# Attention in a fused attention and expert kernel: two heads' scores in row halves, the output scaled in place of P, and a planned order

## The chip, the core and the metric

The kernel runs on one core of a Trainium2 chip. The metric is the device time of one execution in microseconds. The engines are TensorE (PE, with its weight loads PEld), VectorE (DVE), ScalarE (ACT), GpSimd (POOL) and SyncE (SP, which here only issues DMAs).

## What is computed

Block-causal attention over 4 batches of 8 heads, sequence 576, head size 64; then a two-layer softplus network on the 2304 rows, and a routed expert network. Only the first part is touched by the change:

```python
def _attn_ref(q, k, v) -> np.ndarray:
    B, H, S, D = q.shape
    block = 64
    scale = 1.0 / np.sqrt(D)
    scores = scale * np.matmul(q, k.transpose(0, 1, 3, 2))
    ...
    mask = block_i >= block_j
    scores = np.where(mask, scores, -1000000000.0)
    scores = scores - np.max(scores, axis=-1, keepdims=True)
    attn = np.exp(scores)
    attn = attn / (np.sum(attn, axis=-1, keepdims=True) + 1e-09)
    return np.matmul(attn, v).astype(np.float32)
...
    attn_out = _attn_ref(**attn_kwargs)
    x = np.ascontiguousarray(attn_out.transpose(0, 2, 1, 3)).reshape(B * S, H * D)
    x = _moe_ref(x=x, **moe_kwargs)
    return _moe2_ref(x=x, **moe2_kwargs)
```

## The kernel before

Attention works on 16 pairs of heads (`NPAIR`), one pair after the other, overlapped. A pair's q and k come as rows of 128 positions with both heads side by side; `transposes_qk` (L281) turns them with PE into a PSUM tile `tp`, so that head 0 lies on partitions 0 to 63 and head 1 on 64 to 127. `evacuate_qk` (L295) copies them with ACT into `rq` and `rk` (scaling q), and `split_qk` (L306) makes a rounded high part and the remainder, the low part, with ACT, POOL and DVE. The q parts go into `bd`, a block diagonal: for each of the 9 blocks of 64 queries a 128 x 128 matrix with head 0's queries in one corner and head 1's in the other and zeros elsewhere.

`scores` (L376) computes a block's scores for both heads at once, 128 rows (2 heads x 64 queries), with only the keys that the block may see (64 for block 0, 576 for block 8), in three passes (high x high, high x low, low x high) into PSUM tiles `s`, four of one bank each; DVE takes the negated maximum (L389). `exps` (L403) writes P = exp(s - max) with ACT and its row sums; `denominators` and `reciprocals` are small DVE operations; `normalise` (L430) multiplies P by the reciprocals, on DVE for eight blocks and on POOL for block 5. `transposes_p` (L440) turns P with PE into `tp` (three banks), `evacuate_p` (L452) copies it to `pt` with ACT, block 3 with DVE. `values` (L472) multiplies by v: 32-bit matmuls with 64 output rows for each head, head 0 into PSUM partitions 0 to 63 and head 1 into 64 to 127; queries 0 to 255 and 256 to 575 are two halves in one bank each in turn, each computed in two calls. `evacuate_v` (L491) copies the output to `xT` with ACT.

Between these steps each pair converts a piece of the 64-bit expert weights (`convert_piece`, L230: POOL, DVE, ACT) and loads the next.

The order in which instructions are issued is written by hand: `WHEN` gives each step a place in units of a block (nine for a pair), `FIRST` and `LAST` shift single steps of the first three pairs and the last; everything is sorted by place, and each engine executes its instructions in that order. The tile framework adds the semaphore waits. The start of pair 0 has its own functions (`start_first`, L336, with tile 0 alone, and `start_rest`, L349), with filler matmuls (`keep_busy`, L330) between the first transposes: 15, twice 8 and twice 3. At the end `split_x`, `split_w`, `layer1` and `softplus` of the next stage are given places beside the last pair's steps.

## Time and profile before

| | us |
|---|---|
| median of 3 runs (lowest, highest) | 727.8 (725.16, 728.51) |
| the profiled execution | 724.71 |
| its span, first to last instruction | 723.0 |
| PE, DVE, ACT, POOL busy | 691.8, 521.3, 385.8, 268.3 |

The page gives each engine's busy time as a share of the span, the span in 40 slices with the clock granted to PE in tenths of full speed, and groups of instructions by source line. Busy time of PE is a union of overlapping records, so a busy PE need not be at its peak. Time in a stage is better read from distances between starts in the timeline, and idle time from the brackets there, which name what ended it.

### The profile page before, as it was taken

How to read it: one execution, taken by the hardware profiler on the slowest of the kernel's cores; microseconds unless marked ns; L12 is line 12 of the kernel's file. 1: busy time of each engine (PE TensorE's matmuls, PEld its weight loads, DVE VectorE, ACT ScalarE, POOL GpSimd, SP SyncE). 2: the span in 40 equal slices, each digit the busy share in tenths (PEclk: the TensorE clock that was granted, in tenths of full speed). 3: DMA queues.
4: the chain of work that ended last, by engine and by line, in shares of the span. 5: the costliest groups of instructions: out<-in, count | busy, mean ns of one | idle time of the engine just before them, and what ended most of it. 6: DMA issues, size and time to landing. Idle time of an engine off the chain costs nothing. (4 is left out here: it accounts for less than half of the span.)

```text
span 723.0 us, 11570 instructions
## 1 busy us (share of the span) xinstructions
PE 691.8 (96%) x3966; PEld 535.3 (74%) x3966; DVE 521.3 (72%) x1172; ACT 385.8 (53%) x964; POOL 268.3 (37%) x237
## 2 busy tenths in 40 slices
PE   7999999999998999999999999999999999986996
PEld 6777777777766788888888888888888677775742
DVE  6889999999999986568755788667674365574322
ACT  5788888888886565556445344544453232320111
POOL 6567787778757642312121122112110020113220
PEclk8899999999999999999999999999999999999999
DMA  6434252433220110012101011110001140985620
GB/s 155 92 96 97 70 124 66 102 91 91 70 76 27 33 58 30 29 38 67 41 31 58 1 59 59 48 41 29 1 1 52 66 117 1 319 307 167 241 77 11
DMA packets 86197, 56.76 MB, mean 79 GB/s; under 512 B 65102, under 2 KB 74318, under 8 KB 86128
## 3 DMA queue, kind: packets, MB, share of 16 engines
q1 hardware_dynamic: 84832, 53.68, 25.5%
q0 software_dynamic: 1296, 2.24, 1.0%
q8 instruction: 33, 0.54, 0.3%
q14 instruction: 36, 0.29, 0.1%
HBM read 45.11 MB, written 10.92 MB: 78 GB/s over the span
## 5 line engine op out<-in xcount | busy, mean ns | idle before, releaser
L546 PE MATMUL h<-xs,wi 128*128 128x512 f32 (+1 forms) x960 | 215.8, 373 | 1.6 <-DVE xs L527 1.2
L546 PEld LDWEIGHTS h<-xs,wi 128*128 128x128 f32 x960 | 168.5, 188 | 38.0 <-DVE xs L527 1.5
L598 PE MATMUL o<-wo,gh 128*128 128x512 f32 x576 | 182.9, 398 | 0.2 <-DVE wo L535 0.2
L561 DVE SCALAR_TENSOR_TENSOR e<-h,e 128x512 f32<-128x512 f32 (+1 forms) x80 | 50.8, 636 | 103.0 <-ACT e L559 102.4
L598 PEld LDWEIGHTS o<-wo,gh 128*128 128x128 f32 x576 | 106.3, 188 | 23.9 <-DVE wo L535 0.7
L258 POOL TENSOR_TENSOR cc<-cc,cb 128x512 f32<-128x512 f32 (+1 forms) x40 | 44.1, 1101 | 201.9 <-DVE cb L255 157.0
L557 ACT ACTIVATE e<-h 128x512 f32<-128x512 f32 (+1 forms) x80 | 44.3, 553 | 132.3 <-PE h L546 132.3
L598 PE MATMUL o<-wo,gl 128*128 128x512 f32 x288 | 113.9, 396 | 0.0
L411 ACT ACTIVATE p<-s,mx 128x288 f32<-128x288 f32 (+8 forms) x160 | 80.1, 509 | 17.1 <-DVE mx L389 14.1
L434 DVE TENSOR_SCALAR p<-p,sm 128x64 f32<-128x64 f32 (+7 forms) x128 | 77.0, 623 | 0.0
L445 PE MATMUL tp<-ident,p 128*128 128x128 f32 x384 | 70.1, 288 | 5.9 <-DVE p L434 2.9
L389 DVE TENSOR_REDUCE mx<-s 128x1 f32<-128x288 f32 (+8 forms) x160 | 66.3, 442 | 9.0 <-PE s L385 8.9
L567 DVE TENSOR_TENSOR gl<-e,gh 128x512 fp32r<-128x512 f32 (+1 forms) x80 | 65.9, 823 | 6.8 <-DVE gh L566 0.5
L729 POOL DMA_INDIRECT lst<-pay,si x18 | 17.8, 988 | 126.1 <-DVE pay L722 79.3
L598 PEld LDWEIGHTS o<-wo,gl 128*128 128x128 f32 x288 | 54.2, 188 | 13.2
L445 PEld LDWEIGHTS tp<-ident,p 128*128 128x128 f32 x384 | 42.6, 142 | 26.8 <-issue 9.4
L466 ACT ACTIVATE pt<-tp 128x512 f32<-128x512 f32 (+3 forms) x128 | 57.7, 471 | 4.2 <-PE tp L445 4.0
L485 PE MATMUL v<-pt,vr 128*64 128x320 f32 (+4 forms) x448 | 59.3, 374 | 0.5 <-PE s L385 0.5
L566 DVE CAST gh<-e 128x512 fp32r<-128x512 f32 (+1 forms) x80 | 43.8, 547 | 6.7 <-PE o L598 0.5
L558 ACT ACTIVATE e<-e 128x512 f32<-128x512 f32 (+1 forms) x80 | 47.2, 590 | 2.5
L559 ACT ACTIVATE e<-e 128x512 f32<-128x512 f32 (+1 forms) x80 | 47.2, 590 | 2.5
L485 PEld LDWEIGHTS v<-pt,vr 128*64 128x64 f32 (+1 forms) x448 | 25.2, 135 | 23.8 <-issue 12.8
(240 smaller groups left out, 1098.5 us busy)
## 6 DMA issues: line engine op xcount, KB each, us to landing
xs<-in_moe_w_dram SPq DMA_DIRECT2D x16, 512.0 KB, 6.9
raw<-in_moe_w_in_dram SPq DMA_DIRECT2D x12, 512.0 KB, 3.7
raw<-in_moe_w_out_dram SPq DMA_DIRECT2D x12, 512.0 KB, 3.2
xd<-xT SPq DMA_DIRECT2D x18, 256.0 KB, 2.7
out_dram<-xT SPq DMA_DIRECT2D x18, 256.0 KB, 3.5
vr<-in_v_dram SPq DMA_DIRECT2D x32, 128.0 KB, 2.6
qr<-in_q_dram SPq DMA_DIRECT2D x30, 128.0 KB, 3.0
kr<-in_k_dram SPq DMA_DIRECT2D x30, 128.0 KB, 2.6
```

The lines of the kernel that those rows point to most:

```text
L389: nc.vector.tensor_reduce(out=mx[:, si:si + 1], in_=ps[:, 0:e - a], axis=AX.X, op=ALU.max, negate=True)
L411: nc.scalar.activation(out=pn[i][:, a:e], in_=pss[si][:, 0:e - a], func=AF.Exp, bias=nm, accum_out=sm[:, 0, c + si:c + si + 1])
L434: eng.tensor_scalar(out=pt, in0=pt, scalar1=sums[p, g][:, 2, c:c + 1], scalar2=None, op0=ALU.mult)
L445: nc.tensor.transpose(ps[:, j].rearrange("p h q -> p (h q)"), src[:, j * P:(j + 1) * P], ident)
L466: nc.scalar.activation(out=dst, in_=ps[:, 0:nfull], func=AF.Copy)
L485: nc.tensor.matmul(out=ps[h * D:(h + 1) * D, c0 - q0:q1 - q0], lhsT=vt[0:rows, kt, h, :], rhs=rhs, start=(kt == 0), stop=(kt == nk - 1), s ...
L546: nc.tensor.matmul(out=ps[:, 0:n], lhsT=a[:, kc, :], rhs=b[:, 0:n], start=(kc == 0 and j == 0), stop=(kc == KC - 1 and j == 2),)
L558: nc.scalar.activation(out=e[:, 0:n], in_=e[:, 0:n], func=AF.Exp, scale=-1.0)
L559: nc.scalar.activation(out=e[:, 0:n], in_=e[:, 0:n], func=AF.Ln, bias=1.0)
L561: nc.vector.scalar_tensor_tensor(out=g[:, 0:n], in0=ps[:, 0:n], scalar=0.0, in1=e[:, 0:n], op0=ALU.max, op1=ALU.add)
L567: nc.vector.tensor_tensor(out=gl[:, 0:n], in0=g[:, 0:n], in1=gh[:, 0:n].bitcast(F32), op=ALU.subtract)
L598: nc.tensor.matmul(out=acc[c, t], lhsT=a[:, ts], rhs=b, start=(fc == f0 and j == 0), stop=(fc == f1 - 1 and j == 2),)
```

## The change

Queries are taken in four tiles of 128 for one head each, and a tile of 64 + 64 (`TAIL`) for the last 64 queries of both heads.

- **Scores.** For tiles 0 to 3, head 0's matmul uses partitions 0 to 63 (row half one of the array) and head 1's 64 to 127, each with 128 queries, into separate banks of a two-bank PSUM tile; there are two such tiles in place of four single banks, and tile 1 shares that of tile 0. All keys up to the end of the tile are computed; a small bf16 matmul (`unseen` x `ones`) adds -2^33 to the last 64 keys for the first 64 queries. The remainder stays a block diagonal of 64 + 64 queries.
- **Splitting.** `split_high` (ACT) and `split_low` (DVE) read q and k from the PSUM tile; `rq`, `rk` and the POOL and DVE splits go.
- **Scaling.** P is no longer scaled. The reciprocals of a pair (18 columns: high and low parts of 9) are transposed by PE, copied by ACT, spread over 64 partitions each by five matmuls with `spread`, copied by ACT into the place of the output in `xT`, and DVE multiplies the output of P V by them in place of the ACT copy.
- **PSUM.** `tp` has two banks, not three; `va` and `vb` one each for the two halves of P V. P V of the first half is one call.
- **Order.** Steps have costs, needs, buffers and due times; a list scheduler works the order out when the kernel is built. `convert_piece` is cut into five steps, the load of the next piece follows the third. Setup memsets go to POOL; `setup_routing` and the routing loads become steps. The start has 15 filler matmuls and no functions of its own.

```diff
-    ps_t = second.enter_context(tc.tile_pool(name="ps_t", bufs=3, space=PSUM))
+    ps_t = second.enter_context(tc.tile_pool(name="ps_t", bufs=2, space=PSUM))
-    ps_s = first.enter_context(tc.tile_pool(name="ps_s", bufs=4, space=PSUM, side="right"))
+    ps_s = first.enter_context(tc.tile_pool(name="ps_s", bufs=2, space=PSUM, side="right"))
...
-    bd = [[qt_p.tile([P, NB, 2, BLK], F32R, name=f"bd{i}{w}") for w in "hl"] for i in range(2)]
-    kt = [[qt_p.tile([P, S], F32R, name=f"kt{i}{w}") for w in "hl"] for i in range(2)]
-    rq = qt_p.tile([P, S], F32, name="rq")
-    rk = qt_p.tile([P, S], F32, name="rk")
+    TAIL = FULL
+    qs = [[qt_p.tile([P, FULL * P], F32R, name=f"q{i}{w}") for w in "hl"] for i in range(2)]
+    ks = [[qt_p.tile([P, S], F32R, name=f"k{i}{w}") for w in "hl"] for i in range(2)]
+    bd = [[qt_p.tile([P, 2, REM], F32R, name=f"bd{i}{w}") for w in "hl"] for i in range(2)]
+
+    unseen = qt_p.tile([P, P], BF16, name="unseen")
+    UNSEEN = -2.0 ** 33
+
+    spread = pt_p.tile([2 * (2 * FULL + 1), TT, P], F32R, tag="spread", name="spread")
+    NR = 2 * FULL + 1
...
+    def split_of(p, part):
+
+        ps = tq[p, part]
+        (qh, ql), (kh, kl), (bh, bl) = qs[p % 2], ks[p % 2], bd[p % 2]
+        lo, hi = (P, FULL * P) if p == 0 else (0, FULL * P)
+        if part == 0:
+            return [(ps[:, lo:hi], qh[:, lo:hi], ql[:, lo:hi], True)]
+        if part == 1:
+            return [(ps[:, lo:hi], kh[:, lo:hi], kl[:, lo:hi], False)]
+        if part == 3:
+            return [
+                (ps[:, 0:P], qh[:, 0:P], ql[:, 0:P], True), (ps[:, P:2 * P], kh[:, 0:P], kl[:, 0:P], False),
+            ]
+        rows = [slice(h * D, (h + 1) * D) for h in range(2)]
+        return [(ps[r, 0:REM], bh[r, h, :], bl[r, h, :], True) for h, r in enumerate(rows)] + [
+            (ps[:, REM:2 * REM], kh[:, FULL * P:S], kl[:, FULL * P:S], False)
+        ]
+
+    def split_high(p, part):
+        for x, hi, _, is_q in split_of(p, part):
+            nc.scalar.activation(out=hi, in_=x, func=AF.Copy, scale=scale if is_q else 1.0)
+
+    def split_low(p, part):
+        for x, hi, lo, is_q in split_of(p, part):
+            if is_q:
+                nc.vector.scalar_tensor_tensor(
+                    out=lo, in0=x, scalar=scale, in1=hi.bitcast(F32), op0=ALU.mult, op1=ALU.subtract
                 )
-
-    def evacuate_qk(p, part):
-        ps = tq.pop((p, part))
-        if part < 2:
-            nc.scalar.activation(
-                out=(rq, rk)[part][:, 0:FULL * P], in_=ps[:, 0:FULL * P], func=AF.Copy,
-                scale=scale if part == 0 else 1.0,
+            else:
+                nc.vector.tensor_tensor(out=lo, in0=x, in1=hi.bitcast(F32), op=ALU.subtract)
+
+
...
+    def columns(t):
+        return slice(P, 3 * P) if t == 1 else slice(0, (t + 1) * P)
+
+    def scores(p, t):
+        (qh, ql), (kh, kl), (bh, bl) = qs[p % 2], ks[p % 2], bd[p % 2]
+        if t != 1:
+            sc_ps[p, t] = ps_s.tile([P, 2, 512], F32, tag="s", name="s"), st_p.tile([P, 4], F32, tag="mx", name="mx")
+        else:
+            sc_ps[p, 1] = sc_ps[p, 0]
+        ps, mx = sc_ps[p, t]
+        if t == TAIL:
+            for k0, n in ((0, FULL * P), (FULL * P, REM)):
+                for j, (x, y) in enumerate(((bh, kh), (bh, kl), (bl, kh))):
+                    nc.tensor.matmul(
+                        out=ps[:, int(k0 > 0), 0:n], lhsT=x.rearrange("p h q -> p (h q)"), rhs=y[:, k0:k0 + n],
+                        start=(j == 0), stop=(j == 2),
+                    )
+            return
+        cs = columns(t)
+        n = (t + 1) * P
+        last_keys = slice(cs.stop - BLK, cs.stop)
+        heads = [slice(h * D, (h + 1) * D) for h in range(2)]
+        for j, (x, y) in enumerate(((qh, kh), (qh, kl), (ql, kh))):
+            for h, r in enumerate(heads):
+                nc.tensor.matmul(
+                    out=ps[:, h, cs], lhsT=x[r, t * P:(t + 1) * P], rhs=y[r, 0:n], start=(j == 0), stop=False,
+                )
+        for h, r in enumerate(heads):
+            nc.tensor.matmul(out=ps[:, h, last_keys], lhsT=unseen[r, :], rhs=ones[r, 0:BLK], start=False, stop=True)
+
+    def maxima(p, t):
+
+        ps, mx = sc_ps[p, t]
+        if t == TAIL:
+            nc.vector.tensor_reduce(
+                out=mx[:, 0:1], in_=ps.rearrange("p h n -> p (h n)")[:, 0:S], axis=AX.X, op=ALU.max, negate=True
             )
         else:
...
+            c = 2 * int(t == 1)
+            nc.vector.tensor_reduce(
+                out=mx[:, c:c + 2], in_=ps[:, :, columns(t)], axis=AX.X, op=ALU.max, negate=True
             )
 
...
-    def normalise(p, i):
-        g, c = divmod(i, GROUP)
-        pt = pn[i][:, 0:BLK * (i + 1)]
-        eng = nc.gpsimd if i in POOL_NORM else nc.vector
-        eng.tensor_scalar(out=pt, in0=pt, scalar1=sums[p, g][:, 2, c:c + 1], scalar2=None, op0=ALU.mult)
...
+    def exps(p, t, h):
+        ps, mx = sc_ps[p, t]
+        if p not in sums:
+            sums[p] = st_p.tile([P, 2, NR], F32, tag="sm", name="sm", bufs=2)
+        x = ps.rearrange("p h n -> p (h n)")[:, 0:S] if t == TAIL else ps[:, h, columns(t)]
+        c = 2 * int(t == 1) + h
+        nc.scalar.activation(
+            out=pn[t, h], in_=x, func=AF.Exp, bias=mx[:, c:c + 1], accum_out=sums[p][:, 0, 2 * t + h:2 * t + h + 1]
+        )
+
+    rr = {}
+
+    def reciprocals(p):
+
+        sm = sums.pop(p)
+        t = rr[p] = st_p.tile([P, 2 * NR], F32R, tag="rr", name="rr", bufs=2)
+        nc.vector.tensor_scalar(out=sm[:, 1, :], in0=sm[:, 0, :], scalar1=1e-9, scalar2=None, op0=ALU.add)
+        nc.vector.reciprocal(out=sm[:, 0, :], in_=sm[:, 1, :])
+        nc.vector.tensor_copy(out=t[:, 0:NR], in_=sm[:, 0, :])
+        nc.vector.tensor_tensor(out=t[:, NR:2 * NR], in0=sm[:, 0, :], in1=t[:, 0:NR].bitcast(F32), op=ALU.subtract)
+
 
...
+    def rows_of_reciprocals(p):
+        nc.tensor.transpose(pv[p, 0][0:2 * NR, HALF:HALF + P], rr.pop(p).bitcast(F32), ident)
+
+    def keep_rows(p):
+        rs[p] = st_p.tile([2 * NR, P], F32R, tag="rT", name="rT", bufs=2)
+        nc.scalar.activation(out=rs[p], in_=pv[p, 0][0:2 * NR, HALF:HALF + P], func=AF.Copy)
+
+    def spread_reciprocals(p):
+
+        ps = pts[p, "r"] = ps_t.tile([P, 512], F32, tag="tp", name="tp")
+        r = rs.pop(p)
+        for t in range(FULL):
+            nc.tensor.matmul(out=ps[:, t * P:(t + 1) * P], lhsT=spread[:, t, :], rhs=r, start=True, stop=True)
+        nc.tensor.matmul(
+            out=pv[p, 0][:, HALF:HALF + P], lhsT=spread[:, TAIL, :], rhs=r, start=True, stop=True,
+            skip_group_check=True,
+        )
+
+    def x_of(p, q0, q1):
         b, hp = divmod(p, NP)
-        q0, q1 = ((0, HALF), (HALF, S))[half]
-        ps = pv.pop((p, half))
-        nc.scalar.activation(out=xT[:, hp, b * S + q0:b * S + q1], in_=ps[:, 0:q1 - q0], func=AF.Copy)
-
-    POOL_NORM = (5,)
-    DVE_EVAC = (3,)
-    SPLIT = "apv"
+        return xT[:, hp, b * S + q0:b * S + q1]
+
+    def keep_reciprocals(p):
+
+        nc.scalar.activation(out=x_of(p, 0, FULL * P), in_=pts.pop((p, "r")), func=AF.Copy)
+        for h in range(2):
+            r = slice(h * D, (h + 1) * D)
+            nc.scalar.activation(
+                out=x_of(p, FULL * P, S)[r], in_=pv[p, 0][r, HALF + h * REM:HALF + (h + 1) * REM], func=AF.Copy
+            )
+
+    def normalise(p, half):
+        q0, q1 = queries(half)
+        x = x_of(p, q0, q1)
+        nc.vector.tensor_tensor(out=x, in0=pv[p, half][:, 0:q1 - q0], in1=x, op=ALU.mult)
+
+    DVE_EVAC = ((2, 0),)
...
-        for kt in (range(0, nk // 2), range(nk // 2, nk))[part]:
+        for kt in ((range(0, nk),), (range(0, 2), range(2, nk)))[half][part]:
...
-    keep_busy(KBS[0])
+    keep_busy(15)
     make_identity(nc, ident)
-    nc.vector.memset(one, 1.0)
+    nc.gpsimd.memset(unseen, 0.0)
+    for h in range(2):
+        nc.gpsimd.memset(unseen[h * D:h * D + 1, 0:BLK], UNSEEN)
     for i in range(2):
         for w in range(2):
-            (nc.vector, nc.gpsimd)[w].memset(bd[i][w].bitcast(F32), 0.0)
-    for i in range(0, NB - 1, 2):
-        nc.vector.memset(pn[i][:, BLK * (i + 1):BLK * (i + 2)], 0.0)
-    nc.vector.memset(blank[:, :, :, 0], NT)
-    nc.vector.memset(blank[:, :, :, 1], 0)
-    start_first()
-    setup_routing()
-    U = [(p, i) for p in range(NPAIR) for i in range(NB)]
-
-
-    WHEN = {
-        "normalise": [-0.81, -0.02, 0.8, 1.94, 1.97, 3.13, 4.51, 4.77, 7.37],
-        "scores": [-6.89, -6.43, -4.94, -3.99, -2.29, -1.47, -1.32, 0.65, 0.7],
-        "exps": [-5.21, -5.15, -3.6, -1.61, -1.5, -0.44, 2.3, 2.53, 3.31],
-        "transposes_p": [1.22, 1.93, 2.47, 3.48, 4.44, 5.39, 7.03, 7.17, 8.93],
-        "evacuate_p": [2.76, 3.14, 3.74, 4.46, 4.67, 6.89, 8.1, 8.24, 9.45],
-        "join_max": [-5.42, -5.73, -4.17, -3.32, -1.63, -0.68, 1.47, 0.65, 0.87],
-        "denominators": [-3.03, -0.18, 3.44],
-        "reciprocals": [-1.53, 0.23, 3.89],
-        "values": [6.98, 8.34, 10.92, 12.28],
-        "evacuate_v": [9.2, 12.74],
-        "load_qk": [-22.26],
-        "load_v": [-1.76],
-        "transposes_qk": [-19.2, -16.06, -14.87],
-        "evacuate_qk": [-16.53, -14.84, -14.77],
-        "split_qk": [-11.11, -12.62, -8.78],
-        "convert": [1.05, 10.91, 15.45],
+            nc.gpsimd.memset(bd[i][w].bitcast(F32), 0.0)
+
+    nc.gpsimd.memset(zeros, 0.0)
+    nc.gpsimd.memset(blank[:, :, :, 0], NT)
+    nc.gpsimd.memset(blank[:, :, :, 1], 0)
...
+    DUE = {
+        "ldqk": [-30.0], "ldv": [-14.0], "T": [-17.0, -16.0, -15.0, -18.0], "H": [-15.5, -14.5, -13.5, -17.5],
+        "L": [-15.0, -14.0, -13.0, -17.0], "S": [-6.0, -5.5, -4.0, -2.0, 0.0], "M": [-5.5, -5.0, -3.5, -1.5, 0.5],
+        "E": [-5.0, -4.5, -3.0, -1.0, 1.0], "TP": [0.0, 1.0, 2.0, 4.0, 6.0], "EV": [0.5, 1.5, 2.5, 4.5, 6.5],
+        "EV5": [7.0], "V": [3.0, 8.5], "R": [2.0], "RT": [8.5], "RK": [8.6], "RM": [9.0], "RX": [9.2],
+        "N": [10.2, 10.3], "C": [8.0, 9.0, 10.0, 11.0, 12.0],
+
...
+        while could:
+            now = [(t, s) for t, s in ((ready(s, free), s) for s in could) if t is not None]
+            at, best = min(now, key=lambda x: x[0])
+            e = best.parts[0][0]
+            at, best = min(
+                ((t, s) for t, s in now if s.parts[0][0] == e and t <= at + SLACK), key=lambda x: x[1].due
+            )
...
+        for t in range(TT):
+            if t == TAIL:
+                needs = [k("L", i) for i in range(3)]
+                parts = pe(3 * S, b=0.1)
+            else:
+                needs = [k("L", 3)] if p == 0 and t == 0 else [k("L", i) for i in ((3, 0, 1) if p == 0 else (0, 1))]
+                parts = pe(3 * (t + 1) * P + BLK, b=0.15)
+            before = k("S", t - 1) if t else ("S", p - 1, TAIL)
+            if before in steps_of:
+                needs.append(before)
+            add("S", (t,), parts, scores, needs)
+            n = S if t == TAIL else 2 * (t + 1) * P
+            add("M", (t,), dve(n), maxima, [k("S", t)])
+            for h in range(1 if t == TAIL else 2):
+                add("E", (t, h), act(S if t == TAIL else (t + 1) * P, True), exps, [k("M", t)])
...
+        for t in (0, 2, 3, TAIL):
+            ring("s", 2, k("S", t), [e for e in E if e[2] == t or (t == 0 and e[2] == 1)])
...
+        add("R", (), [("DVE", 0.6)], reciprocals, E, args=())
+        add("RT", (), pe(128, 0.86, 0.05), rows_of_reciprocals, [k("R"), k("V", 0, 0)], args=())
+        add("RK", (), act(128), keep_rows, [k("RT")], args=())
+        add("RM", (), pe(576, 0.4535, 0.15), spread_reciprocals, [k("RK"), k("V", 0, 0)], args=())
+        add("RX", (), [("ACT", 0.75)], keep_reciprocals, [k("RM")], args=())
+        add("N", (0,), dve(256), normalise, [k("RX"), k("V", 0, 0)])
+        add("N", (1,), dve(320), normalise, [k("RX"), k("V", 1, 1)])
+        ring("tp", 2, k("RM"), [k("RX")])
+        ring("va", 1, k("V", 0, 0), [k("N", 0), k("RX"), k("EV5")])
+        ring("vb", 1, k("V", 1, 0), [k("N", 1)])
+
...
+    step("spread", [("POOL", 3.0)], setup_spread, (), 5.0)
+    steps_of["RM", 0].needs.append("spread")
+    step("setup", [("POOL", 5.0), ("DVE", 1.0)], setup_routing, (), 12.0)
+    firsts.append("setup")
+    step("load_routing", [("SP", 1.0)], load_routing, ["setup"], PACE + 5.0)
+    step("move", [(None, 0.0)], move_on, firsts + ["load_routing"])
...
+    for kc, (a, b) in enumerate((("DVE", "POOL"), ("DVE", "POOL"), ("DVE", "POOL"), ("DVE", "POOL"))):
+        step(
+            ("x1", kc), [(a, cost_of[a]), (b, cost_of[b])],
+            lambda kc=kc, a=a, b=b: split_x(1, kc, engine[a], engine[b]),
+            [("TP", z) + x for x in of_page[kc]], end + 8 + kc,
+        )
...
+    for s in in_order():
+        s.do()
```

## Rows read from the trace of the kernel before

**Rows 1.** The page, busy us, share of the span and instructions of each engine.
```profile
PE 691.8 (96%) x3966; PEld 535.3 (74%) x3966; DVE 521.3 (72%) x1172; ACT 385.8 (53%) x964; POOL 268.3 (37%) x237
```
**Rows 2.** The page, granted clock in 40 slices of 18 us, tenths of full speed.
```profile
PEclk8899999999999999999999999999999999999999
```
**Rows 3.** Stretches: us, busy us (instructions) of PE, PEld, DVE, ACT, POOL, clock, DMA.
```profile
8.00:16.00 8.00, 6.24 (x30) 5.69 (x30) 4.87 (x11) 4.64 (x18) 4.88 (x4) 0.67 0.81 202
...
24.00:32.00 8.00, 8.00 (x49) 6.54 (x48) 5.43 (x16) 5.67 (x18) 4.15 (x3) 0.76 0.65 142
...
103.10:115.60 12.50, 12.46 (x96) 9.45 (x94) 12.05 (x34) 11.00 (x37) 9.73 (x9) 1.00 0.39 93
...
128.11:141.62 13.51, 12.67 (x96) 9.47 (x94) 12.83 (x36) 10.99 (x37) 9.45 (x9) 1.00 0.36 90
```
**Rows 4.** Timeline, one pair: start us, us, engine, instruction, count, idle before.
```profile
100.31 0.14 PEld L445 LDWEIGHTS tp<-ident,p 128*128 128x128 f32 x1 [0.49 <-DVE p L434]
...
112.81 0.14 PEld L445 LDWEIGHTS tp<-ident,p 128*128 128x128 f32 x1 [0.49 <-DVE p L434]
...
100.83 0.28 PE L385 MATMUL s<-kt1h,bd1h 128*128 128x64 f32 x1
100.94 0.28 PE L385 MATMUL s<-kt1l,bd1h 128*128 128x64 f32 x1
...
101.61 0.28 PE L385 MATMUL s<-kt1h,bd1l 128*128 128x128 f32 x1
101.82 0.27 PE L291 MATMUL tp<-ident,qr 64*128 64x64 f32 x1
101.93 0.22 PE L291 MATMUL tp<-ident,kr 64*128 64x64 f32 x1
102.08 1.34 PE L485 MATMUL v<-pt,vr 128*64 128x320 f32 x12
...
104.40 0.28 PE L385 MATMUL s<-kt1l,bd1h 128*128 128x256 f32 x1
104.52 0.29 PE L385 MATMUL s<-kt1h,bd1l 128*128 128x256 f32 x1
...
110.36 0.39 PE L385 MATMUL s<-kt1h,bd1l 128*128 128x512 f32 x1
110.59 0.29 PE L385 MATMUL s<-kt1h,bd1h 128*128 128x288 f32 x1
...
111.38 0.27 PE L445 MATMUL tp<-ident,p 128*128 128x128 f32 x1
111.58 1.30 PE L485 MATMUL v<-pt,vr 128*64 128x320 f32 x8
```
**Rows 5.** Timeline of PE between 111.55 and 111.69 us alone.
```profile
111.58 0.49 PE L485 MATMUL v<-pt,vr 128*64 128x320 f32 x2
```
**Rows 6.** Timeline of the start, all engines.
```profile
4.52 0.29 DVE L343 COPY rk<-tp 128x128 f32<-128x128 f32 x1 [0.68 <-ACT rq L342]
...
6.88 0.52 PE L354 MATMUL tp<-ident,kr 128*128 128x128 f32 x3 [1.35 <-DMA kr<-in_k_dram]
...
11.17 0.29 PEld L385 LDWEIGHTS s<-kt0h,bd0l 128*128 128x128 f32 x1 [1.29 <-POOL bd0l L324]
```
**Rows 7.** Groups by line: count, busy us, mean ns, idle before (last two: 60 to 200 us).
```profile
L434 DVE TENSOR_SCALAR p<-p,sm 128x64 f32<-128x64 f32 (+7 forms) x128 | 77.0, 623 | 0.0
...
L485 PE MATMUL v<-pt,vr 128*64 128x320 f32 x134 | 22.9, 449 | 0.0
...
L389 DVE TENSOR_REDUCE mx<-s 128x1 f32<-128x512 f32 x12 | 8.1, 673 | 0.0
```
**Rows 8.** Timeline of the end of attention, PE and its weight loads.
```profile
217.84 0.42 PEld L445 LDWEIGHTS tp<-ident,p 128*128 128x128 f32 x4 [0.94 <-DVE p L434]
...
221.29 2.41 PEld L546 LDWEIGHTS h<-xs,wi 128*128 128x128 f32 x11 [1.49 <-DVE xs L527]
...
224.06 2.42 PE L485 MATMUL v<-pt,vr 128*64 128x320 f32 x20
```

More of the change, by code (lines that the diff above doesn't have):

```diff
@@ new lines, in attention_softplus_moe_kernel, with keep_busy @@
+    busy = []
+    def keep_busy(n):
+        if not busy:
+            busy.append(ps_v.tile([P, 512], F32, tag="va", name="busy"))
+        for _ in range(n):
+            nc.tensor.matmul(out=busy[0][:, 0:P], lhsT=ones, rhs=ones, start=True, stop=True)
+    sc_ps = {}
+    sums = {}
+    def columns(t):
[26 more added lines that the diff above has]
+            nc.tensor.matmul(out=ps[:, h, last_keys], lhsT=unseen[r, :], rhs=ones[r, 0:BLK], start=False, stop=True)
@@ L437, in attention_softplus_moe_kernel @@
     pts = {}
+    pv = {}
     HALF = 256
[L440 to L450 removed]
@@ new lines, in attention_softplus_moe_kernel, with __init__, step @@
+    class Step:
+        def __init__(self, parts, do, needs, due):
+            self.parts, self.do, self.needs, self.due = parts, do, needs, due
+            self.takes, self.end = [], None
+    DUE = {
[5 rows of a table added]
+    }
+    steps_of = {}
+    pending = []
+    rings = {}
+    LAT = {"PE": 0.2, "ACT": 0.15, "DVE": 0.15, "POOL": 0.15, "SP": 3.0, None: 0.0}
+    PACE = 10.8
+    SLACK = 0.1
+    def step(key, parts, do, needs=(), due=0.0):
+        s = steps_of[key] = Step(parts, do, list(needs), due)
+        pending.append(s)
+        return s
@@ new lines, in ring, with ready @@
+    def ring(name, size, first, lasts):
+        steps_of[first].takes.append((name, size, lasts))
+    def ready(s, free):
+        t = s.from_
+        for name, size, _ in s.takes:
+            r = rings.setdefault(name, [])
+            if len(r) >= size:
+                for k in r[len(r) - size]:
+                    w = steps_of[k]
+                    if w.end is None:
+                        return None
+                    t = max(t, w.end + LAT[w.parts[-1][0]])
+        e = s.parts[0][0]
+        return max(t, free[e]) if e else t
@@ L1307, in attention_softplus_moe_kernel @@
+    for s in range(2):
+        step(
+            ("l1", s), [("PE", 2.8)], lambda s=s: layer1(s), [("wi", s)] + [("x0", kc) for kc in range(KC)],
+            end + 1 + 3 * s,
+        )
+    step("sp", [("ACT", 1.8), ("DVE", 2.0)], lambda: softplus(0), [("l1", 0)], end + 4)
+    for s in in_order():
+        s.do()
     steps = len(order_of)
```

458 lines of the change are left out of this document (195 added, 263 removed).

## The prediction

> **What bounds the kernel now.** I read the page's busy shares first: TensorE (PE) is busy 96% of the span and no other engine over 72% [rows 1]. A share is only a mean over stages, so next come the stretches: attention fills the first 226 us (the last P V stands at 224.06 for 2.42 us [rows 8]), and the expert stages after it run PE almost without a gap and are not edited. So the change is worth what it changes in the first 226 us, and PE is the engine to count.
>
> Attention is a fixed pattern that repeats once per head pair. The same transpose of P, behind the same wait on VectorE, stands at 100.31 and at 112.81 us [rows 4]: one pair takes 12.50 us. In that wait the weight queue is idle for 0.49 us, so a pair holds some 12.0 us of PE work. VectorE (DVE) is busy 12.05 of these 12.50 us, ScalarE (ACT) 11.00, GpSimd (POOL) 9.73; another pair takes 13.51 us, in which DVE is busy 12.83 [rows 3]. PE and DVE are both full: relief for DVE alone can give back 0.49 us a pair plus that occasional 1 us, about 0.55 us on average, and then PE's own 12.0 us holds. That is why what the change does to PE matters more than the 77 us of DVE work that it deletes.
>
> Before that pattern stands a slow start. The third score pass of pair 0 begins only at 11.17 us, 1.29 us of it waiting for the POOL split [rows 6], and the granted clock is at its lower level (1.2 GHz) for part of 8 to 16 us and of 24 to 32 us, means of 0.67 and 0.76 [rows 2, 3]. At the end PE waits 0.94 and 1.49 us for DVE [rows 8].
>
> **Price of a PE pass.** I price a matmul by the distance from its start to the next start. 64 columns: 0.11 us (100.83 to 100.94). 256 columns: 0.12. 512 columns: 0.23, and six passes of 288 columns take 0.79 (110.59 to 111.38), 0.13 each [rows 4]. So about 0.45 ns a column with a floor of 0.11. A transpose costs 0.11 (101.82 to 101.93).
>
> A change of the array's shape costs something too. From the 128*128 score pass at 101.61 to the 64*128 transpose at 101.82 are 0.21 us, 0.10 over the floor; leaving that shape (101.93 to 102.08) costs 0.15, 0.04 over. Into the 128*64 shape of P V, 111.38 to 111.58, 0.20 us, 0.09 over [rows 4]. Matmuls that write different column halves run together: two of them fit into 0.49 us [rows 5], and 134 records of 449 ns on average, 60 us in series, take 22.9 us of PE [rows 7].
>
> **The scores.** Before, nine blocks with three passes each, the last in two segments: 0.34, 0.33, 0.33, 0.36, 0.43, 0.52, 0.61, 0.69 and six times 0.13 = 0.79, in all 4.4 us a pair. After: four tiles of 128 queries with 128, 256, 384 and 512 keys, each pass for both heads in two row halves, and the remainder as a 128*128 block. No row here shows row halves side by side. The bounds are the column halves, which run fully together, and passes one after the other. I take them as running together, by the nearest row: three times (0.11 + 0.12 + 0.17 + 0.23) = 1.9 us. The two masking matmuls of a tile (64 columns): 0.03 us by the rate, 0.11 at the floor each pair, I take 0.05, so 0.2. Four tiles each go into and out of the half shape: 0.10 + 0.04, and the first weights of a new shape are not hidden, which I estimate at 0.08 (between nothing and the floor of 0.11, and up to twice that where both halves' loads show): 0.22 each, 0.9 in all, bounds 0.14 and 0.34 each. The remainder: three passes of 512 and three of 64 columns, 0.69 + 0.33 = 1.0. Sum 4.0, so 0.4 us less.
>
> That estimate takes the 0.11 floor for 128 columns too, since the 64-column row stands at it. The Trainium skill (TensorE: Matmul & The Clock Gate, Part 3, "What overlaps and what doesn't") says that weight loads overlap running matmuls when their row groups differ; by that rule the short pair passes would go down to the column rate and the sum would be some 0.2 us a pair, 3 us in all, lower. No row here shows it.
>
> **The rest of PE.** The transposes of P stay 25, those of q and k 10 for a pair. P V of the first half becomes one call instead of two, which saves a way into and out of the 128*64 shape: about 0.2 us. New: the transpose of the reciprocals, 0.11, and five matmuls of 18 rows and 128 columns that spread them, 5 x 0.11 and one change of shape, together 0.8 us. Net: -0.4 - 0.2 + 0.8 = +0.2 us, so PE work of 12.2 us a pair. PE is not relieved by this change.
>
> **The other engines.** DVE loses the scaling of P (77 us over 16 pairs, 4.8 us each), the joins, most of the denominators and the cast of k [rows 7]. It gains two low halves of 512 columns out of PSUM, about 0.67 each by the reduce of that size [rows 7], three small ones (0.2 each), two scalings of the output of 256 and 320 columns (0.4 and 0.5) and a wider evacuation (0.15). Its reduces read 3136 columns in 5 instructions instead of 2880 in 10, about 0.4 less. Net roughly -2.5 us, to 9.5 of 12.5. ACT gains the high halves, the row copy and the three reciprocal copies, loses the copies of q, k and v and the narrow evacuations: within 0.5 us of its 11.00, still under PE. POOL loses the splits and keeps three conversions, 2.5 us. All this lies under PE and is worth nothing by itself beyond the 0.49 us.
>
> The waits that the change adds: a transpose bank is now held until both ACT and DVE have read it, with two banks in place of three, so the next transposes queue behind it on PE; and the scores of tile 1 go into the two banks that hold tile 0. The trace shows that users of one bank go one by one: the copy of k at 4.52 waits for the copy of q from the same tile, 0.68 us, though they read different columns [rows 6]. So tile 1's scores wait for tile 0's maximum: last pass visible after some 0.28 us, maximum of 256 columns 0.4, against 0.33 us of transposes that the due times put between. I take 0.2 us, and 0.1 for the transpose banks: 0.3 us a pair in place of 0.55. Bounds: nothing, and 1.0.
>
> Steady state: +0.18 in PE work (the terms above unrounded: -0.41 - 0.24 + 0.83) and -0.25 in waits, some -0.08 us a pair, -1.3 us over 16.
>
> **Start and end.** q and k are split straight from PSUM by ACT and DVE; the POOL step and one copy drop out of the chain. The keys of pair 0 are transposed from 6.88 us [rows 6]; plus transposes 0.5, a high half 0.6 and a low half 0.7, then pair 1's transposes, the scores of tile 1 can begin near 9.4 instead of 11.2: -2 us. Fewer filler matmuls are issued (15 where there were 37), so the lower clock may come sooner; but the chain of pair 0 is shorter and PE fills earlier. I take -1 us for it, with bounds -6 and +4. The memsets moved to POOL stand behind the identity and are not on the path. The routing setup and its loads go later; the piece loads are issued after the read that frees their buffer, so SP's queue holds less. All are hidden by 12 us a pair. At the end, 2.4 us of DVE waits can go, while the reciprocal chain of the last pair is new, only partly hidden by layer 1: -1 us, bounds -3 and +2.
>
> **Sum.** -1.3 - 3 - 1 = -5.3 us. Against the profiled execution (724.71 us, span 723.0) this is 719.4; the median of the runs shown is 727.8, 3.1 us above, and on that footing 722.5. That is barely over 0.5%, about what a measurement of this kernel can tell from no change.
>
> **Rivals.**
> Weights one after the other (slower). If the two heads' weight loads do not overlap, a pair pass costs at least 0.22 us: 3 x (0.11 + 0.10 + 0.05) = 0.8 us a pair, 12.5 us in all: 735. For it: the floor of 0.11 shows loads of 128 columns as the limit. Against: column halves load together [rows 5, 7]. It is slower than before once loads cost 0.33 us a pair more than I take.
> The bank wait grows. If the exps of tile 0 stand before the scores of tile 1 in the bank's order, or DVE is late, PE waits for two exps more, about 0.8 us a pair: 735. For it: the wait at 4.52 [rows 6]. Against: the due times (scores -5.5, exps -5.0) put the scores first. The Trainium skill (PSUM — Partial Sum Buffer, "PSUM bank collisions raise a hardware error") says that two engines must not touch one bank and partition quadrant at once, reads included; the trace agrees (0.68 us at 4.52), so such waits cannot be ordered away.
> The halves do not run together at all: +1.9 us a pair, 30 us: 753. Against it again the column halves.
> Better than taken: change of shape 0.14, waits 0.1, early clock: -0.5 us a pair and 5 us more at the start: 709.
>
> **Chances.** Forecast 0.58 (own range 714 to 731), weights 0.12, bank wait 0.12, no overlap 0.06, better 0.12. Of the forecast 0.34 lies over 0.5% below the median, 0.18 within, 0.06 above. With the better case 0.46 faster; 0.20 same; 0.34 slower. The range leaves out the lower half of the better case with a little of the forecast's tail, and the no-overlap case with the upper tails: 710 to 740.
>
> **What would show it.** The distance between the same transposes of consecutive pairs: 12.5 us if I am right, over 13.2 in the slower rivals, under 12.1 in the better one. Two heads' passes should start within 0.01 us of each other, with 0.11 us (together) or 0.22 us (weights in series) to the next pair pass of tile 0. The wait ahead of tile 1's scores should be near 0.2 us and name DVE. DVE should be near 9.5 us a pair. The first scores of tile 1 should stand near 9.4 us. Wrong would be a PE work per pair over 12.6 or under 11.8, or a start that is later than now.

## The result and the profile after

The changed kernel takes 732.01 us (median of 6 runs, 730.01 to 734.43) where the kernel before, beside it, takes 725.74 us: a ratio of 1.0078, interval 1.0053 to 1.0104. So it is 0.8% slower, where 0.7% faster was forecast. Its profiled execution took 730.01 us, with a span of 727.7; it is the fastest of the six, so the profiles show 4.7 of the 6.3 us between the medians.

The page of the changed kernel (busy us and shares, answering [rows 1]), then two pairs as stretches (columns as in [rows 3]):

```profile
PE 697.1 (96%) x4168; PEld 527.0 (72%) x4168; DVE 474.4 (65%) x981; ACT 382.9 (53%) x932; POOL 156.0 (21%) x177
...
99.63:112.87 13.24, 13.05 (x110) 9.12 (x108) 9.43 (x23) 10.90 (x35) 2.03 (x3) 1.00 0.37 88
112.87:126.10 13.23, 13.04 (x109) 9.11 (x108) 9.42 (x23) 10.88 (x35) 2.03 (x3) 1.00 0.35 87
```

DVE fell from 12.05 to 9.43 us a pair and POOL from 9.73 to 2.03, close to the forecast 9.5 and 2.5. The pair became longer, 13.24 us instead of 12.50, and PE is busy 13.05 us of it (12.46 before). The pair, counted in PE's time from the timelines of both kernels, each block from its first start to the next block's first start:

| us a pair | before | after | measured | forecast |
|---|---|---|---|---|
| scores | 5.04 | 4.19 | -0.85 | |
| transposes of P | 2.86 | 3.58 | +0.72 | |
| both together | 7.90 | 7.77 | -0.13 | -0.41 |
| transposes of q and k | 1.14 | 1.25 | +0.11 | 0 |
| P V | 3.46 | 3.31 | -0.15 | -0.24 |
| reciprocals | 0 | 0.90 | +0.90 | +0.83 |
| pair | 12.50 | 13.23 | +0.73 | -0.08 |
| waits within these rows (measured further down) | 0.24 | 0.33 | +0.09 | -0.25 |

The forecast rows above the pair hold PE's work alone; its forecast waits stand in the last row.

Here is the pair after, as PE's timeline (columns as in [rows 4]):

```profile
99.90 0.87 PE L433 MATMUL tp<-ident,p 128*128 128x128 f32 x6
100.70 0.33 PE L378 MATMUL s<-k1h,q1h 64*128 64x128 f32 x2
100.86 0.28 PE L378 MATMUL s<-k1l,q1h 64*128 64x128 f32 x2
100.98 0.28 PE L378 MATMUL s<-k1h,q1l 64*128 64x128 f32 x2
101.09 0.20 PE L382 MATMUL s<-ones,unseen 64*128 64x64 bf16 x2
101.23 0.55 PE L433 MATMUL tp<-ident,p 128*128 128x128 f32 x3
101.82 0.39 PE L378 MATMUL s<-k1h,q1h 64*128 64x256 f32 x2
102.04 0.28 PE L378 MATMUL s<-k1l,q1h 64*128 64x256 f32 x2
...
102.42 0.55 PE L433 MATMUL tp<-ident,p 128*128 128x128 f32 x3
102.89 0.87 PE L479 MATMUL v<-pt,vr 128*64 128x256 f32 x8
...
105.35 0.20 PE L382 MATMUL s<-ones,unseen 64*128 64x64 bf16 x2
105.70 0.66 PE L303 MATMUL tp<-ident,qr 128*128 128x128 f32 x4
...
106.68 0.27 PE L488 MATMUL v<-ident,rr 128*18 128x128 f32 x1
106.89 0.50 PE L378 MATMUL s<-k1h,q1h 64*128 64x512 f32 x2
...
109.93 1.30 PE L479 MATMUL v<-pt,vr 128*64 128x320 f32 x8
111.16 0.66 PE L499 MATMUL tp<-rT,spread 18*128 18x128 f32 x4
111.66 0.27 PE L500 MATMUL v<-rT,spread 18*128 18x128 f32 x1
111.85 1.35 PE L479 MATMUL v<-pt,vr 128*64 128x320 f32 x12
113.13 0.33 PE L433 MATMUL tp<-ident,p 128*128 128x128 f32 x1
```

The two heads do run together (one row with x2, and 0.12 us from 100.86 to 100.98), so neither rival about the halves came true. What to see is the seams. Three transposes of P between two blocks of scores took 0.25 us in the kernel before:

```profile
103.95 0.49 PE L445 MATMUL tp<-ident,p 128*128 128x128 f32 x3
104.20 0.36 PE L385 MATMUL s<-kt1h,bd1h 128*128 128x256 f32 x1
```

After, three take 0.47 (102.42 to 102.89). At the 0.11 us each by which I had priced a transpose they would take 0.33: the joint before lay 0.08 under that price, the joint after lies 0.14 over it. Before, scores and transposes both had the shape 128*128 and joined without a gap; now each of the four blocks in row halves is a foreign shape between them, and by the forms in the timelines a pair holds 18 changes of shape where it held 11 (an expectation below says 16, which misses two; one more change, into 64*64 at the end of P V, lies inside merged rows of both kernels and is counted in neither). Two waits stand in the weight queue at the same places, naming DVE's maximum and ACT's copy:

```profile
101.82 0.19 PEld L378 LDWEIGHTS s<-k1h,q1h 64*128 64x128 f32 x2 [0.28 <-DVE mx L393]
105.70 0.42 PEld L303 LDWEIGHTS tp<-ident,qr 128*128 128x128 f32 x4 [0.26 <-ACT pt L460]
```

By the distances (0.59 us for the transposes ahead of 101.82 against 0.47 elsewhere; 0.35 us from the mask at 105.35 against 0.14 from that at 101.09) they cost PE 0.12 and 0.21 us, 0.33 in all.

Over the whole execution, with the last 64-row matmuls of a pair's P V as marks: up to pair 4 the kernel gains 4.2 us (86.39 against 90.61), over the nine pairs to pair 13 it loses 6.6 (119.1 against 112.5), from there to the first matmul of layer 2 0.5 more, the experts' middle stage is equal (426.4 and 426.7), and the stretch after the last layer-2 matmul, which nothing edits, is 2.1 us longer (66.3 against 64.2). That adds up to the 4.7 us between the spans.

### The profile page after: what moved, and what is told of

Same layout as the page of the kernel before. It is cut to its first block, busy times and chain, and to the rows that moved or that the text cites. A ratio compares the mean times of both kernels' runs of the same rounds, so it can differ in the third digit from the quotient of the medians.

```text
span 727.7 us, 11608 instructions
## 1 busy us (share of the span) xinstructions
PE 697.1 (96%) x4168; PEld 527.0 (72%) x4168; DVE 474.4 (65%) x981; ACT 382.9 (53%) x932; POOL 156.0 (21%) x177
## 5 line engine op out<-in xcount | busy, mean ns | idle before, releaser
L403 ACT ACTIVATE p<-s,mx 128x128 f32<-128x128 f32 (+2 forms) x144 | 77.9, 547 | 25.1 <-PE s L382 14.0
L393 DVE TENSOR_REDUCE mx<-s 128x2 f32<-128x256 f32 (+1 forms) x64 | 52.5, 822 | 28.9 <-PE s L382 15.7
L433 PE MATMUL tp<-ident,p 128*128 128x128 f32 x384 | 59.9, 287 | 0.8 <-ACT pt L460 0.6
L479 PE MATMUL v<-pt,vr 128*64 128x320 f32 (+4 forms) x448 | 56.0, 370 | 0.2 <-ACT pt L460 0.2
L460 ACT ACTIVATE pt<-tp 128x256 f32<-128x256 f32 (+2 forms) x96 | 49.9, 540 | 11.5 <-PE tp L433 11.5
L433 PEld LDWEIGHTS tp<-ident,p 128*128 128x128 f32 x384 | 41.1, 142 | 7.0 <-issue 2.4
L253 ACT ACTIVATE cc<-raw 128x512 f32<-128x512 uint32 (+1 forms) x40 | 23.2, 580 | 25.0 <-POOL ca L262 24.9
```

The source lines that it names most:

```text
L393: nc.vector.tensor_reduce(out=mx[:, c:c + 2], in_=ps[:, :, columns(t)], axis=AX.X, op=ALU.max, negate=True)
L403: nc.scalar.activation(out=pn[t, h], in_=x, func=AF.Exp, bias=mx[:, c:c + 1], accum_out=sums[p][:, 0, 2 * t + h:2 * t + h + 1])
L433: nc.tensor.transpose(ps[:, at:at + P], pn[t, g][:, j * P:(j + 1) * P], ident)
L460: nc.scalar.activation(out=dst, in_=x, func=AF.Copy)
L479: nc.tensor.matmul(out=ps[h * D:(h + 1) * D, c0 - q0:q1 - q0], lhsT=vt[0:rows, kt, h, :], rhs=rhs, start=(kt == 0), stop=(kt == nk - 1), s ...
```

## The experiments

The question was which of the pair's terms made it longer: changes of shape and added passes (PE's own work) or waits. All distances between pairs are those of the same P V matmuls in consecutive pairs.

**Was the wait that should go there at all?** The kernel before, without the scaling of P:

```diff
     def normalise(p, i):
-        g, c = divmod(i, GROUP)
...
-        eng.tensor_scalar(out=pt, in0=pt, scalar1=sums[p, g][:, 2, c:c + 1], scalar2=None, op0=ALU.mult)
+        pass
```

> The kernel before with the scaling of P left out (so its output lacks the division by the sums; only the stretch of attention is read, from the same transpose of P to the next). It takes about 4.8 us a pair from VectorE and one wait per pair on it. Theory of the prediction (0.49 us of the pair's 12.50 us is PE waiting for VectorE): the pair falls to 12.0 us. Rival (that wait stood in the weight queue while the matmuls of P V still ran, so PE was full): the pair stays within 0.1 us of 12.5 us, and only the odd pairs of 13.5 us may go.

Its pair as a stretch and two rows of PE:

```profile
96.78:109.04 12.26, 12.26 (x95) 9.46 (x93) 7.87 (x25) 10.93 (x37) 7.39 (x8) 1.00 0.40 95
...
99.77 1.09 PE L442 MATMUL tp<-ident,p 128*128 128x128 f32 x8
...
100.62 0.42 PE L385 MATMUL s<-kt1h,bd1h 128*128 128x384 f32 x1
```

The pair fell to 12.26 us, half-way between the two expectations. The P V block whose end carried the 0.49 us bracket lasts 1.23 us in all three kernels (111.58 to 112.81 in [rows 4], 109.93 to 111.16 after): that idle weight queue stood beneath running matmuls and cost nothing. The 0.24 us came from another place, eight transposes that took 1.09 us before and 0.85 here. The bracket there names ACT's split, which ended at 106.53, but the scaling of P on DVE (104.76 for 1.88 us) ended later, at 106.64, and it is the scaling that this run leaves out:

```profile
104.76 1.88 DVE L434 TENSOR_SCALAR p<-p,sm 128x448 f32<-128x448 f32 x2
...
106.08 1.33 PE L445 MATMUL tp<-ident,p 128*128 128x128 f32 x8
...
106.75 0.42 PEld L445 LDWEIGHTS tp<-ident,p 128*128 128x128 f32 x4 [0.25 <-ACT bd0h L317]
...
107.17 0.42 PE L385 MATMUL s<-kt1h,bd1h 128*128 128x384 f32 x1
```

The odd pair of 13.51 us [rows 3] was absent as well.

**Order alone.** The planner's own order, with two of PE's steps moved:

```diff
+    turns_of = [s for s in in_order() if s.parts[0][0] == "PE"]
...
+    for p in range(3, NPAIR - 1):
+        put(("S", p + 1, 1), "after", ("S", p + 1, 0))
+        put(("RM", p), "before", ("V", p, 1, 0))
...
+    for s in in_order(turns_of):
```

> The changed kernel with only the order of PE's instructions edited for pairs 3 to 14: the scores of tile 1 stand right behind those of tile 0, and the spreading of the reciprocals stands ahead of both calls of P V of the second half instead of between them. No instruction is added or taken away. Theory (a pair is PE's work, and each change of the array's shape costs 0.1 us on the way in and 0.05 to 0.1 on the first pass): three changes fewer and the 0.12 us wait of tile 1's scores, the pair falls from 13.23 to about 12.7 us and the time by 5 to 6 us. Rival (the pair is set by waits for ScalarE and VectorE, which this order makes no shorter): the pair falls by at most 0.12 us, the time by less than 1.5 us.

739.74 us, 1.018 of before (1.016 to 1.021); the pair rose to 13.53 us. Rows of PE and DVE around the joint:

```profile
104.87 0.21 PE L382 MATMUL s<-ones,unseen 64*128 64x64 bf16 x2
105.12 0.42 DVE L393 TENSOR_REDUCE mx<-s 128x2 f32<-128x256 f32 x1
...
105.60 0.38 PE L378 MATMUL s<-k1h,q1h 64*128 64x256 f32 x2 [0.52 <-DVE mx L393]
```

Neither expectation: the scores of tile 1, now right behind, still waited for the maximum of tile 0, which reads other columns of the same banks and was issued ahead of them, and without the transposes in between nothing hid it. From the transposes ahead of tile 0 to P V the same instructions took 3.32 us instead of 2.99. Another 0.26 us came behind P V of the first half (1.06 us to the next transposes instead of 0.80), where PE's row (108.06) names DVE's copy of P. The 0.21 us wait at the transposes of q was absent, and the move of the spreading gained about 0.1 us (3.33 instead of 3.41 from the last score pass to the next pair's transposes). Together that is the 0.30 us.

**The remainder in full height.** q, k and P of the remainder are transposed as 128*128 (the last 128 positions of q and k are loaded for it):

```diff
-            n, i = (REM, FULL) if part == 2 else (P, 0)
+            n, i = (P, FULL) if part == 2 else (P, 0)
...
-            nc.tensor.transpose(pv[p, 0][0:REM, HALF + P:HALF + 2 * P], pn[t, 0][:, FULL * P:S], ident)
+            nc.tensor.transpose(pv[p, 0][:, HALF + P:HALF + 2 * P], last_page[:, FULL * P:(FULL + 1) * P], ident)
```

> The changed kernel with the same order, but the transposes of the remainder of q and k take 128 rows (the last 128 positions are loaded, the last 64 used) and the remainder of P is transposed as 128 columns (64 of them zeros), so that both have the 128*128 shape of the instructions around them. The work in columns is the same or more. Theory (changes of shape): three changes fewer, the stretch from the last transposes of P to the remainder's scores shrinks by 0.25 us a pair, the pair falls to 13.0 us, the time by 3 to 4 us. Rival (shape costs nothing, the first pass is slow for another reason): no change, or slower by the extra columns.

729.04 us, 1.004 of before (1.001 to 1.007); the pair 13.11 us. Of the 0.25 us expected 0.12 came: the 0.09 us on the way into the 64-column transpose went, but the first score pass of the remainder still took 0.34 us, now between instructions of one shape, so its length is not the shape's. More columns and less time is on the side of the shapes, at half the size.

**Without the spreading.** The steps `RT`, `RK`, `RM` and `RX` go; the output is scaled by a constant.

> The changed kernel without the transposing, copying and spreading of the reciprocals; the output is scaled by a constant in place of them, so it lacks the division by the sums. Only the stretch of attention is read. Theory (PE's work sets the pair): the transpose 0.11, the five spreading passes 0.56 and the ways into and out of their shape, 0.25, go: the pair falls from 13.23 to about 12.3 us. Rival (another engine or a wait is close behind): the pair stays above 12.9 us.

```profile
94.36:106.39 12.03, 11.81 (x103) 8.35 (x102) 9.54 (x23) 9.91 (x31) 2.04 (x3) 1.00 0.41 97
```

12.03 us, 1.20 less and more than the 0.9 of the passes and their shape: the planner, run anew, also put transposes and P V between tiles 0 and 1, so that the 0.12 us wait went. What else its new order gained or lost was not taken apart. No other engine held the pair at 12.9.

**Two blocks of scores as one step**, so that both maxima are issued behind them (the spreading is moved as in the run with the order alone):

```diff
+            if t == 0 and p:
+                add("S", (t,), pe(9 * P + 2 * BLK, b=0.3), lambda p, t: (scores(p, 0), scores(p, 1)), needs)
```

> The changed kernel with the scores of tiles 0 and 1 as one step for every pair but the first, so that both maxima are issued behind both blocks of scores, and the spreading of the reciprocals ahead of P V of the second half. In the run with only the order edited the scores of tile 1 waited 0.6 us although they stood right behind those of tile 0. Theory: that was the maximum of tile 0, which reads the same banks and was issued ahead of them; with the maxima behind, the wait goes, and two changes of shape (0.25 us), the old wait of 0.12 us and 0.08 us at the spreading are gained: the pair falls from 13.23 to 12.8 us, or to 13.05 us if P V of the first half still waits 0.25 us for a copy behind the maxima. Rival: the scores of tile 1 wait for an earlier reader of the banks: the pair stays at 13.5 us.

```profile
98.61:111.36 12.75, 12.51 (x109) 9.15 (x108) 9.27 (x22) 10.94 (x35) 2.03 (x3) 1.00 0.40 96
...
100.07 0.20 PE L382 MATMUL s<-ones,unseen 64*128 64x64 bf16 x2
...
100.11 0.36 PE L378 MATMUL s<-k1h,q1h 64*128 64x256 f32 x2
```

12.76 us and 724.59 us (1.000, 0.997 to 1.003): the wait was the maximum, and the order of issue removed it. Inside the joined block the mask takes 0.04 us (100.07 to 100.11) where it seemed to take 0.14 ahead of transposes. From the last transposes ahead of tile 0 to the first behind tile 1 the same instructions took 2.61 us instead of 3.00: 0.12 of that is the wait, 0.26 the way out of the half shape and back in.

**What the mask costs.** The masking matmuls left out:

> The changed kernel without the masking matmuls (the last 64 keys of a tile then count for its first 64 queries too, so the output is not that of the reference). It tells what of the 0.135 us between the start of a masking pair and the next instruction is the mask and what is the way out of the half shape. If the mask costs its columns alone (64 columns, 0.04 us, as it stood between two blocks of scores), the way out stays with the last score pass and the pair falls by 4 times 0.04, to about 13.05 us. If the mask costs the 0.135 us, the pair falls by 0.5 us, to 12.7 us.

```profile
101.78:114.89 13.11, 12.87 (x102) 8.74 (x100) 9.38 (x23) 10.87 (x35) 2.04 (x3) 1.00 0.36 88
```

13.11 us, 0.12 less. From the last score pass to the next block it is 0.04 to 0.05 us less at three of the four masks; at the third, whose place is followed by the wait for ACT, nothing (0.53 us with and without it). The rest of the 0.14 us, some 0.09, is the way out of the shape and stays with the last score pass.

**Fewer shapes, then one mask for two tiles.** First the remainder as above and the reciprocals as 128*128 matmuls (zero rows in `rr` and `spread`) ahead of P V; then also one mask for tiles 0 and 1, `RT` ahead of the transposes of q and k, and DVE copying the other head's P of tile 2.

```diff
-        nc.tensor.transpose(pv[p, 0][0:2 * NR, HALF:HALF + P], rr.pop(p).bitcast(F32), ident)
+        nc.tensor.transpose(pv[p, 0][:, HALF:HALF + P], rr.pop(p).bitcast(F32), ident)
...
-    DVE_EVAC = ((2, 0),)
+    DVE_EVAC = ((2, 1),)
```

> The kernel of the run above, with the remainder's transposes at 128 rows and 128 columns, and the reciprocals transposed and spread as 128*128 matmuls (the rows beyond 18 hold zeros): the same number of instructions, 10 changes of the array's shape a pair where the changed kernel has 16. Theory (each change costs 0.1 us in and 0.05 to 0.1 on the first pass): 0.3 to 0.4 us a pair below the run above, the pair at 12.4 to 12.7 us. Rival (another engine's chain holds the pair by now): no more than 0.1 us below the run above.

> The kernel of the run above, with one masking matmul a head for tiles 0 and 1 together (0.13 us a pair less), the transposing of the reciprocals ahead of the transposes of q and k (0.1 us of a wait for ScalarE covered), and the copy of the second head's P of tile 2 on VectorE in place of the first head's (so that ScalarE takes the first one while the maxima run; 0.25 us of a wait). Theory: 12.2 to 12.5 us a pair, the time at 713 to 720 us, below the kernel before (725.8). Rival (ScalarE, busy 10.9 us a pair, and the two transpose banks hold the pair): the pair stays over 12.7 us and the time over 722 us.

```profile
95.31:107.87 12.56, 12.31 (x110) 9.18 (x108) 9.27 (x22) 10.82 (x35) 2.03 (x3) 1.00 0.43 102
```

```profile
95.41:107.78 12.37, 12.29 (x108) 9.10 (x106) 9.29 (x22) 10.87 (x35) 2.04 (x3) 1.00 0.43 100
```

12.56 us and 720.9 us (0.9925, 0.990 to 0.995), then 12.37 us and 718.74 us (0.988, 0.984 to 0.992). Both pairs lie in their expected ranges, but the first step gave 0.20 us where 0.3 to 0.4 was expected: by the rows it takes the changes of shape from 15 to 10, so some 0.04 us for each, as with the three of the remainder alone (0.12 us). A change of shape has no single price here. The second step has three edits, which were not separated. ACT and DVE are as busy as in the changed kernel (10.87 and 9.29 us against 10.90 and 9.43); what went is PE's passes, shapes and waits.

**The scaling put back.** The same kernel, PE's order of a pair held as a list without the reciprocals' steps, with P multiplied by the reciprocals again, on DVE and POOL:

```diff
+    POOL_DIV = ((1, 1), (2, 1), (3, 1))
...
+        eng.tensor_scalar(out=pn[t, h], in0=pn[t, h], scalar1=sums[p][:, 1, c:c + 1], scalar2=None, op0=ALU.mult)
...
-        add("RM", (), pe(576, 0.4535, 0.15), spread_reciprocals, [k("RK"), k("V", 0, 0)], args=())
```

> The kernel with fewer changes of shape and one mask, but with the third part of the change undone: P is multiplied by the reciprocals again, as in the kernel before (six of the nine pieces of P on VectorE, three on GpSimd, which the changed kernel leaves idle for 11 of 13 us), and the transposing, copying and spreading of the reciprocals on PE go; ScalarE copies the output and takes the copy of P that VectorE had. Theory (PE's work sets the pair, and scaling the output costs PE what it saves on VectorE): 0.85 us of PE's work a pair go, the pair falls from 12.37 to about 11.5 us, bounds 11.4 and 12.2 us (VectorE would be busy some 11 us), the time to 703 to 715 us. Rival (VectorE, with the scaling back, sets the pair as the change supposes): 12.4 us a pair or more, no gain over the run above.

```profile
98.89:110.51 11.62, 11.58 (x102) 8.43 (x100) 10.05 (x26) 10.76 (x35) 6.35 (x7) 1.00 0.44 105
```

11.62 us a pair, 715.21 us (0.986, 0.983 to 0.989). DVE, with the scaling back, is busy 10.05 us and does not set the pair. The time, just above the expected 703 to 715, fell less than the pairs because the first pair ended at 39.2 us instead of 33.3:

```profile
23.95 1.09 PE L306 MATMUL tp<-ident,qr 128*128 128x128 f32 x4 [7.82 <-DMA qr<-in_q_dram]
```

So the transposes of pair 2's q were put behind that load:

```diff
+    turns_of.remove(steps_of["T", 2, 0])
+    turns_of.insert(turns_of.index(steps_of["T", 2, 1]), steps_of["T", 2, 0])
```

> The kernel of the run with P scaled again, whose pairs take 11.62 us, but whose first pair ended 6 to 8 us later than that of the other kernels: PE stood 7.8 us at the transposes of pair 2's q, which were ordered ahead of the last scores of pair 0, until their load came. Here these transposes stand behind the third block of scores of pair 1; nothing else is edited. Theory: that wait goes, the last P V of pair 0 stands near 33 us instead of 39.2, the pairs stay at 11.62 us, the time falls by 5 to 7 us to 708 to 711 us. Rival (the start is held by the loads, which PE then meets at its next step): the time falls by less than 2 us.

710.17 us, 0.977 of before (0.973 to 0.981), with the first pair's end at 34.6 us and the same 11.62 us a pair: the version that beats both kernels. Part of the earlier start can be the clock: the first record of it in the trace, at the upper level, stands at 31.8 us in the run before and at 15.2 us here. This version keeps the row halves, the splits from PSUM and the planner, with PE's order of a pair fixed by hand, and leaves out the moved scaling.

## Why the prediction was wrong

- **The wait that goes (wrong, the largest term).** I took 0.49 us of PE idle a pair from the bracket of the weight queue [rows 4], plus an occasional 1 us [rows 3], 0.55 in all. The step that failed is "so a pair holds some 12.0 us of PE work": the stretch says PE busy 12.46 of 12.50 us [rows 3]. Taking the scaling away gave 0.24 us, from another block: 0.31 us less than the 0.55.
- **PE's work (wrong in size).** Without waits it went from 12.26 to 12.90 us (13.23 less 0.33): +0.64, where I had +0.18. The signs of all terms were right. Scores with transposes of P gave -0.22 (7.66 to 7.44 without waits) for -0.41; the transposes of q and k cost 0.11 that I had at nothing; P V gave 0.15 for 0.24; the reciprocals cost 0.90 for 0.83. For the way in and out of a half-shape block I took 0.22 us; joining two blocks gave back 0.26 us, 0.16 us more over four blocks. The joints of the kernel before, which lie below my price of a transpose (0.25 us for three), count on the same side; the two were not told apart. The longer first pass of a block is no part of it: with 256 columns it takes 0.22 us where the next takes 0.12 (101.82, 102.04, 102.16), but 0.20 and 0.12 in the kernel before too (104.20 above, 104.40 and 104.52 in [rows 4]), where the shape stays the same. The mask was right (0.04 to 0.05 for 0.05), the pair passes too (0.12 against 0.11).
- **The bound that I named myself.** "Wrong would be a PE work per pair over 12.6": it is 12.9.
- **New waits (right).** 0.33 us for 0.3, at the two places named: 0.12 for 0.2 at the scores of tile 1, naming DVE as expected, and 0.21 for 0.1 at the transpose banks. Together with the first point: +0.09 for -0.25. That such waits "cannot be ordered away" was wrong: with both maxima issued behind both tiles the first one went.
- **Column rate of the short passes.** The Trainium skill (TensorE: Matmul & The Clock Gate, Part 3, "What overlaps and what doesn't") had weight loads overlap matmuls of other row groups; the short pair passes stayed at 0.11 to 0.12 us (100.86 to 100.98), so here that rule gave nothing.
- **Start (sign right, reason wrong).** The scores of tile 1 began not near 9.4 but at 11.31 us, behind the transposes of the remainder (from 9.07) and of pair 1's q (from 10.29) and at the lower clock (passes 0.22 us apart; a view of the granted clock reads 1.00 there, since the trace has no record of it before 20.25 us). Yet pair 0 ended 6.0 us earlier (31.45 against 37.48). The transposes of P no longer wait for their scaling; the kernel before without the scaling ended pair 0 at 34.05, but with its clock up from 17.5 us on, so the two were not told apart:

```profile
8.55 0.41 PE L378 MATMUL s<-k0l,q0h 64*128 64x128 f32 x2
8.77 0.41 PE L378 MATMUL s<-k0h,q0l 64*128 64x128 f32 x2
...
11.31 0.58 PE L378 MATMUL s<-k0h,q0h 64*128 64x256 f32 x2
...
16.69 1.54 PE L433 MATMUL tp<-ident,p 128*128 128x128 f32 x6
```

  and in the kernel before:

```profile
21.04 0.66 PE L445 MATMUL tp<-ident,p 128*128 128x128 f32 x2 [1.71 <-DVE p L434]
```

  That the clock has a part in it other runs show: with the same order up to pair 2, pair 0 ended at 33.14 and 34.39 us in two of the runs above (full height, order alone), where the lower clock came back between 24 and 32 us.
- **End (wrong sign, small).** Forecast -1, measured +0.5. PE's idle brackets shrank, but all three first blocks of layer 1 now stand behind the last P V (36 matmuls), where one stood ahead of it before (24 behind it):

```profile
226.28 8.88 PE L570 MATMUL h<-xs,wi 128*128 128x512 f32 x36
235.00 0.40 PE L622 MATMUL o<-wo,gh 128*128 128x512 f32 x1
```

```profile
226.41 5.87 PE L546 MATMUL h<-xs,wi 128*128 128x512 f32 x24
232.12 0.40 PE L598 MATMUL o<-wo,gh 128*128 128x512 f32 x1
```

- **The tail (not foreseen, open).** 2.1 us come after the last layer-2 matmul, 1.71 of them one gap of PE that names nothing:

```profile
700.02 1.45 PE L976 MATMUL pye<-wo,hTe 128*128 128x512 f32 x3 [1.71 <-issue]
```

  That stretch took 64.2 us before and 65.1 to 71.1 in the kernels above with the whole computation, though none edits it. The clock does not explain the 2.1 us, since the lower level covers 4.3 us of the stretch after and 5.7 before; in the two longest, 69.8 and 71.1 us, it covers 15.2 and 11.8. What sets the gap was not tried.

The measured pair misses the forecast by 0.81 us: 0.31 from the wait that goes, 0.03 from the new waits and 0.46 from PE's work. The time lies inside the stated 710 to 740, but 1 us outside the forecast's own 714 to 731, in the part of the range that was kept for slower rivals, and those did not come true: that it lies inside is the width of the range and not the mechanism. The direction hung on the sum of small terms of both signs. With 0.24 us for the wait that goes, the pair would have come to +0.24 us, 3.8 us over 16 pairs, against the 4 us taken for start and end: no change. The rest of the slowdown is PE's work.

## What to carry over

Before a wait is counted as a gain, look whether the engine itself stood: an idle weight queue under running matmuls is no idle PE. The busy time of the stretch warns of it (0.04 us idle where the bracket said 0.49) but hid the 0.24 us that were there; the distances between starts show them (1.09 us for eight transposes priced at 0.11). On a PE that is full, count the changes of the array's shape (here 0.26 us out of a row-half block and back in, and some 0.04 us for each change that padding removed): put blocks of one shape side by side, pad odd ones to the shape of their neighbours, and issue the readers of a bank behind all that is written to it. And relief for an engine that does not set the pace is worth nothing if it is paid on the one that does: moving the division to PE's side cost 0.75 us a pair here.
